# Where a decay scan and a reciprocal stand in the VectorE queue: an RWKV-7 recurrence fused with a feed-forward layer

## The chip, the cores and the metric

The kernel runs on one core of a Trainium2 chip. The metric is the device time of one execution in microseconds (us); smaller is better. A core has five engines that work side by side: PE (TensorE, matrix products, with PEld for the loading of its weights), DVE (VectorE), ACT (ScalarE), POOL (GpSimd) and SP, which here only issues transfers (its queue is written SPq). Each engine works through its own list of instructions, and semaphores tie the lists together. Products land in PSUM, from where DVE or ACT fetch them; everything else lies in SBUF.

## The reference, cut to what matters

The inputs `r, k, v, w, a, b` have the shape (4 batches, 8 heads, 768 steps, 40). For every batch and head a 40 x 40 state is carried over the steps; its outputs, 320 per token for 3072 tokens, then go through a feed-forward layer with a hard-swish.

```python
for t in range(S):
    y[:, :, t] = np.einsum('bhd,bhde->bhe', rt, state)
    Sa = np.einsum('bhde,bhe->bhd', state, at)
    state_decay = state * wt[:, :, None, :] - np.einsum('bhd,bhe->bhde', Sa, bt)
    state = state_decay + np.einsum('bhd,bhe->bhde', vt, kt)
...
h = x @ w_in                        # 3072 x 320 by 320 x 2048
g = h * np.clip(h + 3.0, 0.0, 6.0) / 6.0
return (g @ w_out).astype(np.float32)   # by 2048 x 320
```

## The kernel before, in words

**Units.** The sequence is cut in blocks of 64 steps. A unit is one such block of two batches with all 8 heads; there are 24 (`NK`), worked in groups of four (`NU`). Within a block the recurrence is turned into matrix products. A unit has two parts. The part that needs no state, `prepare` (stages W, gam, A, B, F, factor, K, E, EV), is made well ahead; the part that carries the state, `step` (RT, R, VT, S, U, C, UT, rS, sn, H, y, move, move2), follows in order of the units. Once per group a 64 x 64 triangular system is inverted for all 32 heads of the group: `invert` (L648 to L682) is a chain of some 60 DVE operations named prod (L660) and x (L666), each needing the one before, ending in two transposes tb (L669) and tt (L674).

**W and gam.** Stage W turns a block of decays by PE (L420), ACT copies them into `wm` (L480, L481), and one DVE `tensor_tensor_scan` multiplies them up to running products, `prods` (L484). Stage gam then takes the reciprocal of one half of the products on DVE (L495) into `gam`, and three small POOL copies (L496, L497, L499) bring over the rest. Stage A takes a second reciprocal (L510), later.

**The feed-forward layer.** Each unit gives two jobs, r = 0 and r = 1, one for each half of the 2048 features (the first two units are ordered otherwise). A job has two halves: `expand` multiplies by `w_in` into two PSUM banks named h (L974), and `contract` multiplies the result by `w_out` into a bank named o (L1015). Between them stand ACT (L989) and DVE (L990), which make the tiles gt from h. In expand there are 16 wide products, over 128 rows, and 8 short ones, over 64 rows each, for the last 64 of the 320 inputs. The short ones are held back by `narrow`: where `spread[0]` is set they are issued before a certain recurrence product, or else inside the next contract, before the last of its four pieces (`n == LATEST`, after 6 of its 8 products). Only when the short ones are done are the h banks complete, so only then can L989 and L990 begin; and the next expand needs the same two banks.

**The order.** The order of all instructions is written out by hand; the framework adds only the waits. For units from 8 on (`i >= 2 * NU`) the loop is: `a_block` collects the stages that are due and hands them to `together`, which issues all their PE products first, in the order of `PRODUCTS`, and then, in `finish`, all that follows them on the other engines, in the order of `RESULTS` (W and gam stand third and fourth in it, behind RT and y). Then `feed` issues some pieces of the feed-forward layer by `pieces(1)`, and with each of them some operations of the inversion by `aside`. A stage is a generator: its first `yield` separates its products from the rest.

**The end.** When the recurrence is done, `while jobs or next(stream): next(stream)` runs the jobs that are left. With `spread[0]` still set from the loop, the short products of those jobs are issued inside the contract before. A finished unit leaves as a tile ob (L1033, ACT) in two transfers to HBM (L1038, SPq).

Of the kernel before, what the change touches and what calls it, by code (L numbers as in the profile page):

```python
# [17 lines left out]
BL = 64  # L18
# [11 lines left out]
def kernel(  # L30
# [42 lines left out]
    nc = tc.nc  # L73
# [4 lines left out]
    NU = 2 * NP  # L78
# [16 lines left out]
    def bank(tag, shape, bufs):  # L95
        return ps.tile(shape, F32, name=tag, tag=tag, bufs=bufs)
# [11 lines left out]
    def ps_pair(*dims):  # L108
# [19 lines left out]
        out=ident[:], in_=ones, pattern=[[1, P]],  # L128
# [4 lines left out]
        out=ones[:, 0:BL], in_=ones[:, 0:BL], pattern=[[1, BL]],  # L133
# [3 lines left out]
        out=ones[BL:P, 0:BL], in_=ones[BL:P, BL:P], pattern=[[1, BL]],  # L137
# [240 lines left out]

    PE, DONE = 1, 2
    NK = NG * NU
    names = [(2 * (i // NU) + i % NU // NP, i % NP) for i in range(NK)]
    data = [{} for _ in range(NK)]
# [1 line left out]
    def fetch(name, i, engine=None):  # L386

        if i is None or i >= NK:
            return
        x, crossed = {"W": (w, 0), "A": (a, 0), "B": (b, 0), "K": (k, 0), "R": (r, 1),  # L390
                      "V": (v, 1)}[name]
        if name == "V":
            t = values[i % AHEAD]
        else:
            t = (others if i < 2 * NU and i % 2 and name != "R" else inputs)[name]
        g, p = names[i]
        engine = engine or nc.sync
        for q in range(2):
            y = x[2 * p + q, :, g * BL:(g + 1) * BL, :]
            rows = slice(q * BL, (q + 1) * BL)  # L400
            if crossed:
                for s in range(2):
                    engine.dma_start(out=t[rows, 4 * s:4 * s + 4, 0:D],
                                     in_=y[s::2].rearrange("h t e -> t h e"))
            else:
                engine.dma_start(out=t[rows, :, 0:D], in_=y.rearrange("h t e -> t h e"))
        data[i][name + "N"] = t

    def following(i):

        if i < 2 * NU:

            return i + 2 if i % NU < NU - 2 or i % 2 == 0 else None
        return i + 1

    def turn_pairs(x):

        o = ps_any([P, NPR, P])
        for n in range(NPR):
            nc.tensor.transpose(out=o[:, n, :],  # L420
                                in_=x[:, 2 * n:2 * n + 2, :].rearrange("p s e -> p (s e)"),
                                identity=ident[:])
        return o
# [24 lines left out]
    def half(i, n=SLOT):  # L448
        return slice(SLOT * i, SLOT * i + n)
# [21 lines left out]
    def prepare(i, F):  # L471
        n, o = i % NU, data[i]
        halves = i >= 2 * NU
        def w_stage():
            wt = turn_pairs(o["WN"])
            yield PE

            wv = wm[:].rearrange("p (r m i) -> p r m i", m=2, i=HB + 1)
            x = wt[:].rearrange("p r (q m i) -> p (r q) m i", q=2, m=2)
            nc.scalar.activation(out=wv[:, :, 0, 1:HB + 1], in_=x[:, :, 0, ::-1], func=AF.Copy)  # L480
            nc.scalar.activation(out=wv[:, :, 1, 1:HB + 1], in_=x[:, :, 1, :], func=AF.Copy)  # L481
            fetch("W", following(i))
            prods = o["prods"] = tmp.tile([P, NB, 2, HB + 1], F32, name="prods", bufs=2)
            nc.vector.tensor_tensor_scan(  # L484
                out=prods[:].rearrange("p r m i -> p (r m i)"), data0=wm[:], data1=start[:],
                initial=0.0, op0=ALU.mult, op1=ALU.add,
            )

        def gam_stage():

            gam = o["G"] = grp.tile([P, NPR, P], F32, name="gam", tag="gam", bufs=NU + 2)
            rgam = o["rg"] = tmp.tile([P, NPR, P], F32, name="rgam", bufs=2)
            gv = gam[:].rearrange("p r (q i) -> p (r q) i", q=2)
            rv = rgam[:].rearrange("p r (q i) -> p (r q) i", q=2)
            nc.vector.reciprocal(gv[:, :, 0:HB], o["prods"][:, :, 0, 1:HB + 1][:, :, ::-1])  # L495
            nc.gpsimd.tensor_copy(gv[:, :, HB:BL], o["prods"][:, :, 1, 0:HB])  # L496
            nc.gpsimd.tensor_copy(rv[:, :, 0:HB], o["prods"][:, :, 0, 0:HB][:, :, ::-1])  # L497
            dec = grp.tile([P, 2, 2, NPR], F32, name="dec", tag="dec", bufs=NU + 2)
            nc.gpsimd.tensor_copy(dec[:].rearrange("p m q r -> p r q m"),  # L499
                                  o["prods"][:].rearrange("p (r q) m i -> p r q m i", q=2)[:, :, :, :, HB])  # L500
            o["dec"] = dec
            if i <= 2 * NU:
                fetch("V", i)
            yield from ()
# [434 lines left out]
    narrow, spread, LATEST = [], [False], 2  # L939
# [67 lines left out]
    def contract(i, r, gts):  # L1007
        split = i < SPLIT
        if r == 0 or split:
            op = bank("o", [P, DM], 1)  # L1010
        else:
            op = sums.pop(i)
        for c in range(2):
            for n in range(NQ):
                nc.tensor.matmul(out=op[:], lhsT=gts[c][:, n, :],  # L1015
                                 rhs=wout[:, c * HJ + r * NQ + n, :],
                                 start=((split or r == 0) and c == 0 and n == 0),
                                 stop=((split or r == 1) and c == 1 and n == NQ - 1))
                if n % 2 and (c == 0 or n < NQ - 1):
                    yield True  # L1020
        if r == 0:
            sums[i] = op
            if split:
                part = ffn.tile([P, 3 * P], F32, name="part", tag="xt", bufs=6)[:, 0:DM]
                nc.scalar.activation(out=part, in_=op[:], func=AF.Copy, scale=1.0 / 6.0)
                sums[i] = part
        else:
            ob = ffn.tile([P, DM], F32, name="ob", bufs=OB)
            if split:
                nc.vector.scalar_tensor_tensor(out=ob[:], in0=op[:], scalar=1.0 / 6.0,  # L1030
                                               in1=sums.pop(i), op0=ALU.mult, op1=ALU.add)
            else:
                nc.scalar.activation(out=ob[:], in_=op[:], func=AF.Copy, scale=1.0 / 6.0)  # L1033
            del ready[i]
            g, p = names[i]
            for q in range(2):
                row = (2 * p + q) * T + g * BL
                nc.sync.dma_start(out=out[row:row + BL, :], in_=ob[half(q)])  # L1038
        yield True


# [6 lines left out]
    def pieces(n):  # L1048

        owed[0] += n * (8 / 9 if spread[0] else 1)  # L1050
        while owed[0] >= 1:
            owed[0] -= 1
            if not next(stream):
                owed[0] = 0.0

    def aside(n, weight=0):

        for _ in range(n):
            if side and next(side[0], side) is side:
                side.popleft()  # L1060
            due[0] += weight
            while due[0] >= 1:
                due[0] -= 1
                next(weights, None)
# [116 lines left out]
    for line in PLAN:  # L1181
        plan.append([])
        while line:
            i = line.popleft()
            if i != "T":
                i = int(i)
# [50 lines left out]
    BLOCKS = 4  # L1237
    FIRST_NARROW = PRODUCTS[len(TURNS)]

    def together(stages):  # L1240

        begun, banks = [], 0

        def finish():
            begun.sort(key=lambda x: RESULTS.index(x[0]))
            for _, rest in begun:
                for _ in rest:
                    pass
            begun.clear()
            shared[0] = None  # L1250

        for name in PRODUCTS:
            if name == FIRST_NARROW and narrow and spread[0] and stages:
                narrow[0]()
            for stage in stages.get(name, []):
                if name in TURNS:
                    need = 1
                else:
                    width = WIDTH.get(name, NPR * BL)
                    need = 2 * (shared[0] is None or shared[1] + width > 512)  # L1260
                if banks + need > 5:
                    finish()
                    banks, need = 0, 1 if name in TURNS else 2
                banks += need
                rest = stage()
                next(rest)
                begun.append((name, rest))
        begun.extend((name, stage()) for name in stages if name not in PRODUCTS
                     for stage in stages[name])
        finish()  # L1270
# [26 lines left out]
    def feed(n, inversion):  # L1297

        whole = int(n)
        for k in range(whole):  # L1300
            pieces(1)
            aside(inversion)
        pieces(n - whole)

# [25 lines left out]
    for _ in range(2):  # L1330
        for _ in a_block(m):
            pass
        m += 1
    while jobs or next(stream):
        next(stream)

# [29 lines left out]
```

## Time and profile before

Three runs gave 831.4 us in the median (829.04 to 831.72). The profiled execution took 831.98 us; its span, from the first to the last instruction, is 830.2 us.

| what | value | how to read it |
|---|---|---|
| PE busy | 746.4 us, 90% of the span | matrix products, their ends modelled |
| DVE busy | 547.4 us, 66% | includes the inversion chains |
| ACT, POOL busy | 321.7 us, 156.1 us | 39% and 19% |
| PE busy, 360 to 790 us | 425.44 of 430 us | the steady part |
| DVE busy, 360 to 790 us | 258.71 of 430 us | the steady part |
| scan L484 | 24 times, 1254 ns each | one a unit |
| reciprocal L495 | 24 times, 1741 ns each | one a unit |
| gt on ACT L989, on DVE L990 | 96 times each, 686 and 677 ns | two a job |
| wide h products L974 | 2304 records, mean 284 ns | each fp32 product leaves two records; wide and short mixed; pipelined, so these overlap |

The sixteen units whose preparation the loop issues (8 to 23) have their scans between 264.26 and 633.2 us. Before 240 us the kernel loads and converts weights, and PE is often idle; that stretch is not touched by the change.

### The profile page before, as it was taken

To read this page: it belongs to the slowest core of one execution; us is meant where nothing else is said; L and a number is where in the kernel's file an instruction comes from. 1 tells how busy PE (TensorE), PEld (TensorE's weight loads), DVE (VectorE), ACT (ScalarE), POOL (GpSimd) and SP (SyncE) were. 2 spreads that over 40 slices of the span, in tenths; PEclk is the share of its full clock that TensorE was granted. 3 is DMA by queue.
4 is the path that set the end of the run, shared out by engine and by line. 5 is a ranking of instruction groups with operands and counts; after the bars stand their busy time and mean duration, and the time that the engine had idled before them with its cause. 6 is when DMAs were issued, how large, how long until landed. Compare 5 with 4: busy or idle time off the path is not lost.

```text
span 830.2 us, 35843 instructions
## 1 busy us (share of the span) xinstructions
PE 746.4 (90%) x15832; PEld 632.0 (76%) x15832; DVE 547.4 (66%) x1108; ACT 321.7 (39%) x864; POOL 156.1 (19%) x305
## 2 busy tenths in 40 slices
PE   4732877898999999999999999999999999999997
PEld 3622766686887878788888888878888888888875
DVE  7999697988964769844589654799556685232201
ACT  1323744232344533454433635334553334322211
POOL 3231301122112230321220222112212102000000
PEclk7755587999999999999999999999999999999999
DMA  7573344331133230322331332232232101100000
GB/s 141 85 187 85 91 113 100 70 62 25 21 59 65 52 66 19 59 46 48 56 51 28 60 62 44 42 58 36 45 60 48 22 20 29 29 20 16 15 18 16
DMA packets 174218, 45.05 MB, mean 54 GB/s; under 512 B 157424, under 2 KB 172784, under 8 KB 174064
## 3 DMA queue, kind: packets, MB, share of 16 engines
q1 hardware_dynamic: 171920, 42.44, 26.8%
q8 instruction: 125, 2.05, 1.0%
q10 hardware_dynamic: 2144, 0.33, 0.2%
q14 instruction: 29, 0.24, 0.1%
HBM read 34.08 MB, written 3.93 MB: 46 GB/s over the span
## 4 chain that ended last, share of the span: by engine, by line
PE 70%; DVE 12%; issue 9%; ACT 3%; POOL 2%; DMA 1%; SPq 0%; POOLq 0%; DVEq 0%; ACTq 0%
PE h L974 24%; PE o L1015 22%; PE any L458 4%; PE any L889 3%; PE any L420 2%; PE any L430 2%; PE any L865 2%; DVE prod L660 2%; DVE x L666 2%; PE any L770 1%; PE any L809 1%; DVE parts L320 1%; PE any L830 1%; PE any L846 1%; PE any L696 1%
## 5 line engine op out<-in xcount | busy, mean ns | idle before, releaser
L974 PE MATMUL h<-xt,win 128*128 128x128 f32 (+1 forms) x2304 | 252.8, 284 | 7.0 <-DVE gt L990 7.0
L974 PEld LDWEIGHTS h<-xt,win 128*128 128x128 f32 (+1 forms) x2304 | 232.5, 193 | 25.8 <-issue 8.8
L1015 PE MATMUL o<-wout,gt 128*128 128x320 f32 x768 | 232.8, 445 | 0.2 <-DVE gt L990 0.2
L1015 PEld LDWEIGHTS o<-wout,gt 128*128 128x128 f32 x768 | 139.0, 191 | 51.2 <-issue 1.4
L989 ACT ACTIVATE gt<-h,three 128x512 f32<-128x512 f32 x96 | 62.1, 686 | 104.6 <-PE h L974 104.4
L990 DVE SCALAR_TENSOR_TENSOR gt<-gt,h 128x512 f32<-128x512 f32 x96 | 61.5, 677 | 61.2 <-ACT gt L989 61.2
L660 DVE TENSOR_TENSOR prod<-x 128x30 f32<-128x30 f32 (+9 forms) x180 | 62.8, 349 | 13.5 <-POOL x L651 8.1
L904 POOL TENSOR_TENSOR yg<-ys,gam 128x512 f32<-128x512 f32 x22 | 39.1, 1778 | 167.9 <-DVE ys L902 121.9
L874 DVE TENSOR_TENSOR state<-any,state 40x160 f32<-40x160 f32 (+1 forms) x88 | 27.9, 321 | 62.7 <-PE any L865 36.3
L666 DVE TENSOR_TENSOR x<-x,prod 128x30 f32<-128x30 f32 (+9 forms) x180 | 65.2, 362 | 5.4
L590 POOL TENSOR_TENSOR KBt<-K,rgt 128x320 f32<-128x320 f32 x24 | 21.1, 880 | 248.1 <-ACT rgt L580 217.3
L467 DVE COPY_PREDICATED score<-mask,any 128x256 f32<-128x256 int32 x143 | 53.4, 436 | 4.0 <-PE any L458 3.6
L495 DVE RECIPROCAL gam<-prods 128x256 f32<-128x256 f32 x24 | 41.5, 1741 | 13.5 <-POOL yg L904 13.2
L510 DVE RECIPROCAL rgam<-prods 128x256 f32<-128x256 f32 x24 | 41.8, 1741 | 0.0
L484 DVE TENSOR_TENSOR_SCAN prods<-wm,start 128x528 f32<-128x528 f32 x24 | 30.1, 1254 | 16.6 <-ACT wm L481 14.9
L623 ACT ACTIVATE EV<-any 64x160 f32<-64x160 f32 x92 | 24.8, 295 | 39.8 <-PE any L617 30.3
L902 DVE TENSOR_TENSOR ys<-any,ys 128x256 f32<-128x256 f32 x44 | 16.6, 418 | 34.1 <-PE any L617 18.3
L749 ACT ACTIVATE RT<-any 128x256 f32<-128x256 f32 (+1 forms) x44 | 15.5, 400 | 49.6 <-PE any L430 49.5
L889 PE MATMUL any<-score,KBt 64*64 64x64 f32 x1536 | 31.2, 232 | 2.4 <-DVE score L467 1.6
L889 PEld LDWEIGHTS any<-score,KBt 64*64 64x64 f32 x1536 | 27.5, 144 | 5.3 <-DVE score L467 1.7
L729 ACT ACTIVATE tinv<-any 32x256 f32<-32x256 f32 (+1 forms) x56 | 19.3, 344 | 28.9 <-PE any L719 28.1
L775 DVE TENSOR_TENSOR RR<-any,EV 128x160 f32<-128x160 f32 x44 | 12.2, 318 | 25.6 <-PE any L458 25.4
(193 smaller groups left out, 1077.4 us busy)
## 6 DMA issues: line engine op xcount, KB each, us to landing
B<-in_b_dram SPq DMA_DIRECT2D x48, 80.0 KB
K<-in_k_dram SPq DMA_DIRECT2D x48, 80.0 KB
V<-in_v_dram SPq DMA_DIRECT2D x96, 40.0 KB
out_dram<-ob SPq DMA_DIRECT2D x48, 80.0 KB
R<-in_r_dram SPq DMA_DIRECT2D x92, 40.0 KB
W<-in_w_dram SPq DMA_DIRECT2D x40, 80.0 KB
A<-in_a_dram SPq DMA_DIRECT2D x40, 80.0 KB
xt<-yg SPq DMA_DIRECT2D x72, 40.0 KB
```

The costliest lines, as they stand in the source:

```text
L458: nc.tensor.matmul(out=o[i][half(q), n, :], lhsT=lhs[half(i, D), n ^ (2 * q * swap), half(q)], rhs=rhs[half(i, D), n, half(q)], start=True ...
L467: nc.vector.copy_predicated(out=x[:, 4 * i:4 * i + 4, :], mask=mask4, data=o[i])
L495: nc.vector.reciprocal(gv[:, :, 0:HB], o["prods"][:, :, 0, 1:HB + 1][:, :, ::-1])
L510: nc.vector.reciprocal(rv[:, :, HB:BL], o["prods"][:, :, 1, 1:HB + 1])
L660: nc.vector.tensor_tensor(out=pv, in0=_ap(x[:], (i + 1) * L + i, [[L, n], [0, i]]), in1=_ap(x[:], i * L, [[0, n], [1, i]]), op=ALU.mult,)
L666: nc.vector.tensor_tensor(out=rest, in0=rest, in1=pv, op=ALU.add)
L889: nc.tensor.matmul(out=y[q][half(s), pr, :], lhsT=o[name][half(q), h * D:h * D + SLOT], rhs=m[name][half(q), 4 * rs + 2 * s + j, :], start ...
L904: nc.gpsimd.tensor_tensor(out=yg[:], in0=m["ys"][:].rearrange("p r q t -> p r (q t)"), in1=o["G"][:], op=ALU.mult)
L974: nc.tensor.matmul(out=hp[c][:, i, :], lhsT=lhsT, rhs=rhs, start=(begun[c] == 0), stop=(begun[c] == 3 * NQ - 1))
L989: nc.scalar.activation(out=gt[:], in_=hp[c][:], func=AF.Relu, bias=three[:], scale=1.0)
L990: nc.vector.scalar_tensor_tensor(out=gt[:], in0=gt[:], scalar=6.0, in1=hp[c][:], op0=ALU.min, op1=ALU.mult)
L1015: nc.tensor.matmul(out=op[:], lhsT=gts[c][:, n, :], rhs=wout[:, c * HJ + r * NQ + n, :], start=((split or r == 0) and c == 0 and n == 0), ...
```

## The change

Three edits. First, for units from 8 on, stage W yields a new mark LATER ahead of the scan, and stage gam yields it ahead of its reciprocals and copies. `finish` then lays the rest of the stage aside in `deferred`, and `later()` issues it either after the next `pieces(1)` in `feed` or at the start of the next `together`. Second, `spread[0]` is set to False ahead of the last loop, so that expand issues the 8 short products of a job right behind its 16 wide ones there. Third, the second half of the last unit's output is issued from the ACT queue and no longer from SPq.

```diff
-    PE, DONE = 1, 2
+    PE, DONE, LATER = 1, 2, 3
...
         def w_stage():
...
             fetch("W", following(i))
+            if i >= 2 * NU:
+                yield LATER
             prods = o["prods"] = tmp.tile([P, NB, 2, HB + 1], F32, name="prods", bufs=2)
             nc.vector.tensor_tensor_scan(
...
         def gam_stage():
 
             gam = o["G"] = grp.tile([P, NPR, P], F32, name="gam", tag="gam", bufs=NU + 2)
+            if i >= 2 * NU:
+                yield LATER
             rgam = o["rg"] = tmp.tile([P, NPR, P], F32, name="rgam", bufs=2)
...
             for q in range(2):
                 row = (2 * p + q) * T + g * BL
-                nc.sync.dma_start(out=out[row:row + BL, :], in_=ob[half(q)])
+                queue = nc.scalar if q and i == NK - 1 else nc.sync
+                queue.dma_start(out=out[row:row + BL, :], in_=ob[half(q)])
...
+    deferred = deque()
+
+    def later():
+
+        while deferred:
+            for _ in deferred.popleft():
+                pass
+
     def together(stages):
 
+        later()
         begun, banks = [], 0
 
         def finish():
             begun.sort(key=lambda x: RESULTS.index(x[0]))
             for _, rest in begun:
-                for _ in rest:
-                    pass
+                for at in rest:
+                    if at == LATER:
+                        deferred.append(rest)
+                        break
             begun.clear()
             shared[0] = None
...
         for k in range(whole):
             pieces(1)
+            later()
             aside(inversion)
         pieces(n - whole)
...
+    spread[0] = False
     while jobs or next(stream):
         next(stream)
```

## The prediction, made before the changed kernel was run

> **What bounds the kernel now.** I read the page first: busy shares, then the 40 slices.
>
> ```profile
> PE 746.4 (90%) x15832; PEld 632.0 (76%) x15832; DVE 547.4 (66%) x1108; ACT 321.7 (39%) x864; POOL 156.1 (19%) x305
> PE   4732877898999999999999999999999999999997
> PEclk7755587999999999999999999999999999999999
> ```
>
> PE is full from the tenth slice on, and at full clock. The change touches units 8 to 23 and the end, so only stretches from about 264 us on count. There PE leaves little: 425.44 of 430 us are busy between 360 and 790 us. A gain can only come from PE's idle time, so next I read the waits of PE alone, 240 to 790 us (columns: total us, times, longest).
>
> ```profile
> PE h L974 <- DVE gt L990: 3.6, 3, 1.3
> PE any L458 <- issue: 3.1, 4, 1.0
> PE any L696 <- ACT wm L481: 1.3, 1, 1.3
> PE any L617 <- issue: 1.1, 1, 1.1
> PE any L770 <- DVE score L467: 0.7, 1, 0.7
> PE any L846 <- DVE score L467: 0.2, 1, 0.2
> ```
>
> All of PE's idle time here is 10.6 us. 3.6 + 0.7 + 0.2 = 4.5 us of it waits for DVE; the "issue" rows wait for nothing that the profile shows. The timeline gives the places: L974 idles 1.29, 1.15 and 1.14 us at 308.82, 431.95 and 549.70 us, L770 0.73 us at 312.74, L846 0.20 us at 285.72. The second of them, in the timeline from 426 us:
>
> ```profile
> 426.49 0.75 DVE L902 TENSOR_TENSOR ys<-any,ys 128x256 f32<-128x256 f32 x2
> 427.15 1.25 DVE L484 TENSOR_TENSOR_SCAN prods<-wm,start 128x528 f32<-128x528 f32 x1
> 427.31 2.15 POOL L904 TENSOR_TENSOR yg<-ys,gam 128x512 f32<-128x512 f32 x1 [5.01 <-DVE ys L902]
> 427.95 1.24 ACT L989 ACTIVATE gt<-h,three 128x512 f32<-128x512 f32 x2
> 429.50 1.75 DVE L495 RECIPROCAL gam<-prods 128x256 f32<-128x256 f32 x1 [1.10 <-POOL yg L904]
> 431.17 1.22 DVE L990 SCALAR_TENSOR_TENSOR gt<-gt,h 128x512 f32<-128x512 f32 x2
> ```
>
> The reader is to see that ACT has both gt ready by 429.19, but that DVE reaches them at 431.17: scan, 1.10 us of waiting for POOL's yg, and reciprocal stand ahead. PE waits for the h bank which the first gt frees.
>
> The end is the third view, the timeline from 799 us:
>
> ```profile
> 799.53 1.16 PE L974 MATMUL h<-xt,win 64*128 64x128 f32 x16
> 800.62 1.34 PE L1015 MATMUL o<-wout,gt 128*128 128x320 f32 x4
> 800.73 1.27 ACT L989 ACTIVATE gt<-h,three 128x512 f32<-128x512 f32 x2 [7.40 <-PE h L974]
> 801.44 1.29 DVE L990 SCALAR_TENSOR_TENSOR gt<-gt,h 128x512 f32<-128x512 f32 x2 [11.51 <-ACT gt L989]
> 802.18 3.65 PEld L974 LDWEIGHTS h<-xt,win 128*128 128x128 f32 x32 [0.73 <-DVE gt L990]
> 802.19 3.84 PE L974 MATMUL h<-xt,win 128*128 128x128 f32 x32 [0.22 <-DVE gt L990]
> ```
>
> Behind the short products PE has only 4 records of contract left (about 1.1 us) to cover ACT and DVE, and so waits for the h bank. The same stands at 811.84 us, and at 821.50 us ahead of the last contract.
>
> [...]yg takes 2.15 us beside the scan, but 1.27 us at 787.61 us beside a gt, which has one input in PSUM. [...]the two last transfers start at 826.62 and 827.13 us, and SP's waits for them end at 828.66 and 829.29 us, 2.04 and 2.16 us later.
>
> **The change part by part: the scan.** First what moves. I compared the order of instructions on each engine in both programs. On DVE it differs in five places alone: in two (units 8 and 9) a pair of score copies (L467) comes ahead of scan and reciprocal, in three (units 10, 14 and 18, while an inversion runs) the pair gt L990. For the other eleven units nothing stood between the old place and the new. PE differs in the last three jobs only, POOL nowhere, ACT and SP by the last transfer. POOL's copies L496, L497 and L499 keep their place but wait for the later scan; who needs them (stage A, scale) comes over 8 us later.
>
> - *264 us, unit 8.* DVE would do the scores (0.71 us) when their product ends, about 263.9, in what is now idle time, and the scan 0.3 us later than now. PE has no wait on DVE there (its 0.97 us at 267.14 is "issue"). Gain 0; at most that 0.97.
> - *282 us, unit 9.* The scores come 3 us earlier, and L846's 0.20 us goes. gt starts within 0.1 us of now. PE is the bound until the inversion starts, so I take 0.2, between 0 and 0.2.
> - *304 us, unit 10.* gt's ACT ended at 303.16, so DVE does gt at 304.13, then the scan at 305.35; yg, now beside gt, needs some 1.3 to 1.5 us and is through at about 306, so the reciprocal's wait of 1.09 us shrinks to 0 to 0.25. PE's 1.29 us goes. But what is late next is DVE: from 308 to 343.4 us it runs the inversion without a gap, PE already waits for its score at 312.74, and PE's 1.28 us at 345.27 hangs on the end of the inversion through ACT's L681. So the gain is what DVE gains, 0.85 to 1.09, not 1.29 + 0.73. I take 0.9.
> - *427 us, unit 14.* Here gt's ACT is late: its first half ends at about 428.6. DVE now idles from 427.2 to 428.65 (1.45 us) where it idled 1.10, and then needs gt 1.2, scan 1.25, reciprocal 1.75: the inversion goes on at about 432.8 where it was 432.31, 0.47 us later. PE is released at once and starts 1.15 us earlier, at 430.8. Then it meets the later DVE: L549 at 443.04 needs bt, which ended at 441.58 (margin 1.46; PE 1.15 earlier plus DVE 0.47 later is 1.62, so 0.15 to 0.2 is lost); h at 445.87 needs the gt which ended at 444.65 (margin about 1.1 after 0.1 of signalling, so only 0.6 of PE's lead survives); L696 at 463.61 needs the wm copy which ended at 462.81 and stands on ACT behind the inversion's L681 (margin 0.75: PE's lead can be no more than 0.75 − 0.47 = 0.28). I take 0.3, between 0.25 and 1.15, the upper end if those bounds do not bite.
> - *545 us, unit 18.* The same picture with the same numbers (idle 1.10 and 1.14): 0.3.
>
> Sum: 0 + 0.2 + 0.9 + 0.3 + 0.3 = 1.7 us.
>
> **The short products at the end.** From the chain of waits, a job's PE work there is 3.57 (32 wide records) + 1.14 (16 short) + 16 × 0.269 = 4.31 (contract; 12 take 3.23), together 9.02 us. The period is 811.84 − 802.19 = 9.65 us. With the short ones right behind the wide ones, the whole contract, 4.31 us, lies over ACT and DVE, which need about 2.0 us (800.73 to 802.73). So 0.63 us go at each of two boundaries. At the third, PE's last contract starts 0.22 us after a wait and runs from 821.31 by the chain, 4.85 us with its tail where 4.31 + 0.16 would do, and its predecessor ended at 821.13: 0.6 to 0.7 more. Laid end to end from 792.64: 3 × 9.02 + 4.31 = 31.37, so 824.0 where the last product now ends at 826.07. Gain 2.0 us, between 1.5 and 2.1. The contract adds one wait, for ACT's ob to free the o bank; in the new order wide and short products, 4.7 us, cover it. The short products need the third part of xt. The transfers issued at 792.00 are for unit 23, whose first job is the second of the three; PE comes to its short products at about 805, so nothing is lost.
>
> **The last transfer.** Both halves now start at about the end of ob; the later one started 0.51 us behind. ACT's issue of a transfer was 0.6 to 0.7 us long early in this trace, against 0.47 to 0.60 on SP, so I take 0.5, between 0.3 and 0.6.
>
> Total 1.7 + 2.0 + 0.5 = 4.2 us. Against the profiled execution (831.98, that is a span of 830.2 and 1.8 around it) it gives 827.8. That execution lies 0.58 us above the median of the runs; from 831.4 the forecast is 827.2 us.
>
> **Rivals.** *All waits on DVE go* (4.5 us) with the whole of the end (2.5): 7.0, 824.4 us. For it: the waits are real and are named by the profile. Against it: 0.73 at 312.74 and the margins above; DVE has no gap during inversions. *Only the end gains* and the steady part gives everything back: 2.5, 828.9 us; that would also be the case if the deferral did nothing, which the order of instructions already denies for five of sixteen units. *Slower:* [...]gt now stands with its own wait ahead of scan, reciprocal and inversion. Each us by which ACT's gt comes later than 428.6 delays the inversion by as much, in the three groups of 304, 427 and 545 us. For 0.3% on the slower side the three would have to lose 4.2 + 2.5 = 6.7 us, 2.2 us each beyond the 0.47 counted: about 834.5 us. For it: ACT has four EV copies (1.11 us) ahead of gt. Against it: these start at 426.94, before anything moved, so nothing delays them further.
>
> **How the numbers follow.** About 0.3%, 2.5 us, is what a measurement of this kernel can tell from no change; the three runs spread over 2.7 us. Chances: forecast 0.58, all waits 0.17, only the end 0.18, slower 0.07. The forecast's own bounds are 0 to 0.97 + 0 to 0.2 + 0.85 to 1.09 + twice 0.25 to 1.15, with 1.5 to 2.1 and 0.3 to 0.6, so 3.2 to 7.3 us, or 824.1 to 828.2. Down to 823.5 takes in "all waits" with run-to-run spread, up to 830.0 "only the end" likewise. Faster means below 828.9: nearly all of the first case and the second, under half of the third, some lost to the spread: 0.75. Same: 0.19. Slower: 0.06.
>
> **What would show it.** PE's row "h L974 <- DVE gt L990" gone from the steady part; DVE's first prod or x after the gt at 431.2 coming some 0.5 us later relative to its ys, while PE comes 1.15 earlier; L549, h or L696 then showing new waits on DVE or ACT; yg at 1.3 to 1.5 us in three places; a period of 9.0 us at the end; the two last transfers starting together. Wrong it would be if L696 shows no wait and PE keeps 1.15 us at each place, if DVE waits longer for gt than 1.5 us, or if PE's "issue" waits, 4.8 us here, change their number.

## The result, and the profile after

Fifteen runs of each kernel gave 828.73 us in the median against 832.11 us. The ratio to before, estimated over all these runs and not the quotient of the two medians, is 0.9966 (95% interval 0.9953 to 0.9979), a gain of 2.8 us (1.7 to 3.9). The profiled execution took 827.57 us, its span 825.9 us against 830.2. So the changed kernel is faster, by two thirds of the 4.2 us forecast.

The change moved the code down by a few lines: the scan is L486, the reciprocal L499, h L978, gt L993 and L994, contract L1019, the inversion L664 and L670, tinv's copies L685, the third block's products L700 and L723. Here are the waits of PE in the changed kernel, 240 to 790 us (total, times, longest):

```profile
PE any L458 <- issue: 2.9, 3, 1.3
PE any L774 <- DVE score L467: 1.4, 1, 1.4
PE any L700 <- ACT wm L481: 1.3, 1, 1.3
PE any L621 <- issue: 1.1, 1, 1.1
PE any L850 <- DVE bt L525: 0.9, 2, 0.4
PE any L813 <- issue: 0.5, 1, 0.5
PE any L458 <- ACT UT L841: 0.3, 1, 0.3
```

The row of L974 for gt, 3.6 us before, is gone. What waits for DVE now is L774 at unit 10 (1.4, was 0.7) and, new, L850 for bt, once behind unit 14 and once behind unit 18. DVE's share fell from 4.5 to 2.3 us (1.4 + 0.9). But PE's waits are not all that counts, as the next view shows: four stretches of the changed kernel, cut at the steps of PE's clock (columns: length, PE busy, PEld, DVE, ACT, POOL, granted clock, DMA share, GB/s).

```profile
336.11:339.52 3.41, 3.41 (x127) 3.30 (x122) 3.41 (x2) 1.71 (x2) 1.99 (x3) 1.00 0.32 53
339.52:342.93 3.41, 2.09 (x75) 1.74 (x74) 2.55 (x5) 3.36 (x13) 2.57 (x4) 1.00 0.53 99
342.93:346.35 3.42, 3.42 (x42) 2.97 (x41) 2.48 (x3) 3.20 (x8) 2.05 (x6) 0.50 0.29 48
346.35:349.76 3.41, 3.41 (x88) 2.43 (x88) 2.82 (x6) 0.00 (x0) 0.00 (x0) 1.00 0.52 87
```

PE is fully busy from 342.93 to 346.35, but at half clock (0.50): 42 records, where the two other full stretches shown hold 127 and 88. I call PE's lead the time by which a record of PE starts earlier than the same record does in before. It falls there by 1.17 us, from 3.74 to 2.57. Before had no half clock at all between 200 and 830 us.

A sum over one pair of profiles misleads for another reason. I cut every trace of this study at the same instructions: start-up (to the first product of `any<-at,kt` after 255 us, at 262.89 us in before), steady part (to the first wide product of the last three jobs), end (to the end of the last product), and out (from the end of the last ob to the end of the span). About 0.5 us between end and out is the ob itself.

| profile | start-up | steady | end | out | half clock in the steady part, at |
|---|---|---|---|---|---|
| before | 262.89 | 529.74 | 33.44 | 3.64 | none |
| after | 260.50 | 529.54 | 31.97 | 3.34 | 342.9 |
| after_again | 262.60 | 528.56 | 31.97 | 3.33 | 344.5 |
| tail_only | 263.28 | 531.34 | 31.97 | 3.34 | none |
| tail_again | 263.50 | 531.36 | 31.97 | 3.33 | none |
| defer_only | 261.95 | 528.71 | 33.44 | 3.63 | 344.0 |
| defer_8_to_13 | 263.00 | 528.87 | 31.97 | 3.33 | 311.9 |
| gam_only | 262.74 | 525.32 | 31.97 | 3.33 | 344.7 |
| gam_only_again | 262.77 | 524.99 | 31.97 | 3.33 | 344.9 |
| gam_from_14 | 261.14 | 528.83 | 31.97 | 3.34 | none |
| gam_late_tinv | 264.39 | 525.36 | 31.97 | 3.33 | none |
| late_tinv_again | 262.84 | 524.41 | 31.97 | 3.33 | none |

2.4 of the 4.3 us between the first two spans lie in the start-up, which the change doesn't touch and which varies by 3.9 us over these profiles. The end and the last transfer repeat to 0.01 us: 1.47 and 0.30. The steady part of before happens to be the lowest of three with the same order (530.8 in the mean); four with the deferral, of units 8 to 13 at least, have 528.9. By these the change is worth 1.9 + 1.47 + 0.30 = 3.7 us, within the interval; with 1.6 us between steady parts of the same order, this is rough.

### The profile page after: what moved, and what is told of

Same layout as the page of the kernel before. It is cut to its first block, busy times and chain, and to the rows that moved or that the text cites. A ratio compares the mean times of both kernels' runs of the same rounds, so it can differ in the third digit from the quotient of the medians.

```text
span 825.9 us, 35844 instructions
## 1 busy us (share of the span) xinstructions
PE 744.1 (90%) x15832; PEld 631.8 (77%) x15832; DVE 547.3 (66%) x1108; ACT 320.8 (39%) x864; POOL 153.2 (19%) x305
## 4 chain that ended last, share of the span: by engine, by line
PE 67%; DVE 12%; issue 11%; ACT 4%; POOL 2%; DMA 2%; SPq 1%; POOLq 0%; DVEq 0%; ACTq 0%
PE h L978 22%; PE o L1019 22%; PE any L458 4%; PE any L893 3%; PE any L430 2%; PE any L420 2%; PE any L869 2%; DVE prod L664 2%; DVE x L670 2%; PE any L774 1%; PE any L813 1%; DVE parts L320 1%; PE any L834 1%; PE any L700 1%; PE any L850 1%
## 5 line engine op out<-in xcount | busy, mean ns | idle before, releaser
L978 PE MATMUL h<-xt,win 128*128 128x128 f32 (+1 forms) x2304 | 251.6, 283 | 3.0 <-DVE gt L994 3.0
L978 PEld LDWEIGHTS h<-xt,win 128*128 128x128 f32 (+1 forms) x2304 | 232.4, 192 | 19.0 <-issue 4.2
L1019 PE MATMUL o<-wout,gt 128*128 128x320 f32 x768 | 232.2, 446 | 0.0
L1019 PEld LDWEIGHTS o<-wout,gt 128*128 128x128 f32 x768 | 139.5, 192 | 51.2 <-issue 1.4
L994 DVE SCALAR_TENSOR_TENSOR gt<-gt,h 128x512 f32<-128x512 f32 x96 | 61.6, 677 | 59.4 <-ACT gt L993 59.3
L993 ACT ACTIVATE gt<-h,three 128x512 f32<-128x512 f32 x96 | 62.0, 685 | 96.0 <-PE h L978 95.7
L664 DVE TENSOR_TENSOR prod<-x 128x30 f32<-128x30 f32 (+9 forms) x180 | 62.7, 348 | 13.5 <-POOL x L655 8.1
L670 DVE TENSOR_TENSOR x<-x,prod 128x30 f32<-128x30 f32 (+9 forms) x180 | 65.1, 362 | 5.4
L908 POOL TENSOR_TENSOR yg<-ys,gam 128x512 f32<-128x512 f32 x22 | 36.5, 1658 | 165.7 <-DVE ys L906 99.6
L499 DVE RECIPROCAL gam<-prods 128x256 f32<-128x256 f32 x24 | 41.5, 1741 | 10.5 <-POOL yg L908 9.9
L486 DVE TENSOR_TENSOR_SCAN prods<-wm,start 128x528 f32<-128x528 f32 x24 | 30.2, 1258 | 7.7 <-ACT wm L481 6.0
```

The costliest lines, as they stand in the source:

```text
L664: nc.vector.tensor_tensor(out=pv, in0=_ap(x[:], (i + 1) * L + i, [[L, n], [0, i]]), in1=_ap(x[:], i * L, [[0, n], [1, i]]), op=ALU.mult,)
L670: nc.vector.tensor_tensor(out=rest, in0=rest, in1=pv, op=ALU.add)
L908: nc.gpsimd.tensor_tensor(out=yg[:], in0=m["ys"][:].rearrange("p r q t -> p r (q t)"), in1=o["G"][:], op=ALU.mult)
L978: nc.tensor.matmul(out=hp[c][:, i, :], lhsT=lhsT, rhs=rhs, start=(begun[c] == 0), stop=(begun[c] == 3 * NQ - 1))
L993: nc.scalar.activation(out=gt[:], in_=hp[c][:], func=AF.Relu, bias=three[:], scale=1.0)
L994: nc.vector.scalar_tensor_tensor(out=gt[:], in0=gt[:], scalar=6.0, in1=hp[c][:], op0=ALU.min, op1=ALU.mult)
```

## The experiments

**The two halves.** `tail_only` takes the two `yield LATER` out of the changed kernel, `defer_only` takes the other two edits out.

```diff
--- tail_only against after (the same in gam_stage)
-            if i >= 2 * NU:
-                yield LATER
--- defer_only against after
-    spread[0] = False
...
-                queue = nc.scalar if q and i == NK - 1 else nc.sync
-                queue.dma_start(out=out[row:row + BL, :], in_=ob[half(q)])
+                nc.sync.dma_start(out=out[row:row + BL, :], in_=ob[half(q)])
```

> The end alone: the short products of the last three jobs at once and the second output half from ACT, no deferral. Theory 1 (the deferral is worth about 1.4 us, the end 1.8): 1.8 us below before, ratio 0.9978; in the trace the stretch from the wide products of the first of the three jobs to the last product takes 32.0 us against 33.4, and the steady part shows before's three waits of L974 for gt, about 1.2 us each. Theory 2 (the deferral is worth all of the 4.5 us of waits): also 0.9978, but then the full change must stand at 0.993. Theory 3 (the deferral is worth nothing): the full gain, 2.8 us, ratio 0.9966.

> The deferral alone, with the end as before. Theory 1: 1.4 us below before, ratio 0.9983, with steps of PE's lead of about +0.5 at unit 9, +0.9 at unit 10 and 0 across units 14 and 18. Theory 2: 4.5 us, ratio 0.9946. Theory 3: 1.000. If the 3.4 us at half the PE clock that the changed kernel's trace shows near 342 us belong to the deferral, they are here again and the ratio is about 0.9997.

Measured: tail_only 0.995 (0.9933 to 0.9968, from 6 runs), more than its trace can hold; defer_only 0.9981 (0.9968 to 0.9995, 18 runs). Because of that contradiction tail_only ran again:

> tail_only once more, since its first ratio, 0.995, is below what its trace accounts for (1.8 us, 0.9978). If the trace is right, the two together come nearer to 0.9978; if it is not, they stay at 0.995 and this trace shows a gain elsewhere.

It gave 0.9981 (0.9971 to 0.999, 22 runs): this fits the trace's 1.8 us. The first ratio was then a lucky sample of six; short start-ups are the likely reason, but the runs without a profile don't show theirs. The product of the two halves, 0.9981 × 0.9981 = 0.9962, agrees with the change; with both tail runs weighted by their number it is 0.9955, which still lies in the change's interval. The timeline of tail_only at the end shows how the end's 1.47 us come about:

```profile
794.62 4.83 PE L974 MATMUL h<-xt,win 128*128 128x128 f32 x48
799.37 4.58 PE L1015 MATMUL o<-wout,gt 128*128 128x320 f32 x16
799.48 1.27 ACT L989 ACTIVATE gt<-h,three 128x512 f32<-128x512 f32 x2 [4.17 <-PE h L974]
800.19 1.29 DVE L990 SCALAR_TENSOR_TENSOR gt<-gt,h 128x512 f32<-128x512 f32 x2 [8.28 <-ACT gt L989]
```

ACT and DVE are through at 801.48, and the contract that covers them lasts to 803.9; no idle time stands ahead of any product.

**Units 14 and 18.** `defer_8_to_13` leaves the deferral away from unit 14 on.

```diff
-            if i >= 2 * NU:
+            if 2 * NU <= i < 14:
                 yield LATER
```

> The changed kernel with the deferral only for units 8 to 13. Theory 1 (at units 14 and 18 the deferral is worth nothing): the same time as the changed kernel within 0.3 us, with before's waits of 1.15 us of L974 for gt back at both places and no steps of PE's lead across them, and the half clock near 342 us again. Theory 2 (0.3 us or more at each): 0.6 us or more above the changed kernel.

Measured: 0.9966 (0.9953 to 0.9979), the same as the change. The two waits of L978 for gt are back (2.3 us together) and the time isn't worse, so removing them at units 14 and 18 is worth nothing that these runs can tell; their interval is 1.1 us to either side. The traces say the same more sharply, as the next paragraph shows. Its half clock came at another place, which is taken up below.

**Why they are worth nothing.** The timeline of the changed kernel at unit 14:

```profile
423.90 0.75 DVE L906 TENSOR_TENSOR ys<-any,ys 128x256 f32<-128x256 f32 x2
424.73 1.27 POOL L908 TENSOR_TENSOR yg<-ys,gam 128x512 f32<-128x512 f32 x1 [5.00 <-DMA R<-in_r_dram]
425.36 1.24 ACT L993 ACTIVATE gt<-h,three 128x512 f32<-128x512 f32 x2
426.07 1.28 DVE L994 SCALAR_TENSOR_TENSOR gt<-gt,h 128x512 f32<-128x512 f32 x2 [1.42 <-ACT gt L993]
427.27 1.25 DVE L486 TENSOR_TENSOR_SCAN prods<-wm,start 128x528 f32<-128x528 f32 x1
428.62 1.75 DVE L499 RECIPROCAL gam<-prods 128x256 f32<-128x256 f32 x1
430.29 0.33 DVE L670 TENSOR_TENSOR x<-x,prod 128x220 f32<-128x220 f32 x1
```

DVE stands idle for 1.42 us until ACT's gt is there, and the inversion (L670) goes on 6.39 us after ys began; before it was 432.31 − 426.49 = 5.82. PE's lead rises by 1.39 us at h and is then spent on a DVE that is 0.57 us late. At L850 0.97 us of it go, 0.45 as idle time ahead of the first record and the rest among its records:

```profile
438.76 0.74 DVE L525 TENSOR_TENSOR bt<-any,rgam 128x256 f32<-128x256 f32 x2
439.23 0.96 PE L850 MATMUL any<-RT,S 40*64 40x64 f32 x29 [0.45 <-DVE bt L525]
```

In before the same two stood so:

```profile
440.83 0.74 DVE L521 TENSOR_TENSOR bt<-any,rgam 128x256 f32<-128x256 f32 x2
442.57 0.65 PE L846 MATMUL any<-RT,S 40*64 40x64 f32 x32
```

That is a margin of 0.99 us between the end of bt (441.58) and L846, and 1.39 + 0.57 − 0.99 = 0.97. The rest, 0.44 us, goes at the first of the third block's products (L700), which wait for ACT's wm and the next copy, both standing behind tinv's copies. Behind them the lead over before is 2.53 us; ahead of unit 14 it was 2.57. At unit 18 the steps are 1.37 up, then 0.98 and 0.40 down.

If so, DVE's idle 1.42 us is the place for the scan, which takes 1.25 and needs nothing that is late. `gam_only` leaves the scan where it was and defers only stage gam:

```diff
--- gam_only against after, in w_stage
-            if i >= 2 * NU:
-                yield LATER
             prods = o["prods"] = tmp.tile([P, NB, 2, HB + 1], F32, name="prods", bufs=2)
```

> The changed kernel with the scan left where it was and only gamma's reciprocal and copies deferred. Theory 1 (at units 14 and 18 DVE stands idle 1.4 us for ACT's gt and so resumes the inversion 0.5 us late): the scan, 1.25 us, fills that idle time, the inversion resumes 0.7 to 0.8 us earlier than in before, and PE keeps 0.7 to 1.1 us at each of the two units; together 1.4 to 2.0 us below the changed kernel, about 0.994 of before. Against it: at unit 9 the scores stand behind the scan again, up to 0.3 us back. Theory 2: the same time as the changed kernel within 0.3 us, since gt was not late there. Theory 3: the same as tail_only.

> gam_only once more, beside gam_late_tinv on the same chip, to see which of the two is the faster and whether the half-clock stretch near 342 us comes back. By the traces so far: half clock again behind the wait at the third block, 1.1 us of PE's waits for DVE left, 0.992 to 0.994 of before.

Measured: 0.9923 (0.9904 to 0.9942), and again 0.9934 (0.992 to 0.9948): about 3 us faster than the change, more than the 1.4 to 2.0 expected. The timeline of gam_only at unit 14:

```profile
424.55 0.75 DVE L904 TENSOR_TENSOR ys<-any,ys 128x256 f32<-128x256 f32 x2
425.21 1.25 DVE L484 TENSOR_TENSOR_SCAN prods<-wm,start 128x528 f32<-128x528 f32 x1
426.72 1.29 DVE L992 SCALAR_TENSOR_TENSOR gt<-gt,h 128x512 f32<-128x512 f32 x2 [0.26 <-ACT gt L991]
427.92 1.75 DVE L497 RECIPROCAL gam<-prods 128x256 f32<-128x256 f32 x1
429.58 0.32 DVE L668 TENSOR_TENSOR x<-x,prod 128x220 f32<-128x220 f32 x1
```

Idle 0.26 us and no longer 1.42; the inversion goes on 5.03 us after ys, 0.8 us sooner than before. PE wins 1.39 and 1.38 us at h at the two units and keeps practically all of it, and it waits for DVE 1.1 us in the whole steady part. The expectation took only DVE's 0.8 us for what PE would keep; PE kept more. Of PE's lead at unit 10 gam_only keeps about 0.3 us more than the change, and at unit 9 it loses nothing; why it keeps more at unit 10 stays open.

**The half clock.** The changed kernel once more:

> The changed kernel once more. If the 3.4 us at half the PE clock near 342 us are a matter of the moment, this trace lacks them or has them elsewhere, and PE's lead over before across units 10 to 12 stays at about 0.9; if they belong to the change, they are at the same place and cost 1.2 us again. PE's lead at 262 us, ahead of anything that the change moves, was 2.4 us in the first trace; if it is the state of the start-up alone, it differs here by 1 us or more. Time: 0.9966 of before, give or take 0.0013.

Measured: 0.9959 (0.9944 to 0.9974). The start-up was 2.1 us longer than in the first trace. The half clock was there again behind the same wait of PE for wm at L700, and in defer_only and both gam_only too; in the three traces with the old order it was not.

In the traces of before and after, all 19 changes of the granted clock in each lie whole multiples of 3.413 us apart, to within 0.001 us; in the changed kernel, for one, half clocks begin at 192.74 and at 342.93 us, 44 times 3.413 us apart. Carried on through a trace, these times are a grid; I call its parts of 3.41 us clock stretches and its lines edges. In the clock stretch ahead of the half clock (339.52 to 342.93 above) PE was busy for 2.09 us, 61%.

If the place of the idle time within a clock stretch matters, the lead won at unit 10 has moved the idle 1.3 us to another place. `gam_from_14` is gam_only with `if i >= 14` in gam_stage, so that nothing is shifted there; `gam_late_tinv` is gam_only with the wait itself taken away, by issuing tinv's copies behind the first half of the third block:

```diff
             yield
-            nc.scalar.activation(out=tinv[z:z + L, :, 0:L], in_=tb[z:z + L], func=AF.Copy)
+            copies.append((z, tb))
             nc.gpsimd.tensor_copy(tinv[z + L:z + BL, :, L:BL], tb[z + L:z + BL])
...
         yield DONE
+        for z, x in copies:
+            nc.scalar.activation(out=tinv[z:z + L, :, 0:L], in_=x[z:z + L], func=AF.Copy)
+        copies.clear()
         tp = ps_pair(H, L)
```

> As gam_only, but only for units from 14 on; units 8 to 13 as in before, so that nothing shifts PE against the clock's 3.41 us stretches around 345 us. Clock theory (the half-clock stretch after 342 us comes because the lead won at unit 10 moves PE's idle 1.3 us ahead of L696's third-block products to another place within a stretch): no half clock in the steady part of this trace, no gain at units 9 and 10, 1.3 us kept at each of units 14 and 18, and the end's 1.8: 4.4 us below before, ratio 0.9947. Rival (the half clock belongs to the deferred reciprocal as such, wherever it is): a half-clock stretch at 460 or 580 us, and 1.2 us less.

> gam_only with the two ACT copies tinv<-tb, 2.1 us, issued only ahead of the second half of the third block, so that the wm copies of the next unit no longer stand behind them. Clock theory: PE's wait of 1.29 us at the third block near 345 us goes, and with it the half-clock stretch behind it (1.2 us): 2.4 us below gam_only, about 0.9895 of before. Rival (the half clock has another cause): the wait goes, the half clock stays, 1.2 us below gam_only. If the copies are late for the U products, L809 shows a new wait on ACT and the gain shrinks by it.

> gam_late_tinv once more. Clock theory: no half clock in the steady part again, 1 to 2.4 us below gam_only_again. Rival (its first trace lacked the half clock by chance): half clock in this trace, and no more than 1.2 us below gam_only_again.

Measured: gam_from_14 0.9935 (0.9916 to 0.9954), no half clock, and 1.30 of the 1.39 us of lead won at unit 14 kept. gam_late_tinv 0.9908 (0.9887 to 0.993) and again 0.992 (0.9904 to 0.9935), no half clock in either. From the waits of PE in its second trace:

```profile
PE any L777 <- DVE score L467: 1.1, 1, 1.1
PE any L619 <- issue: 1.1, 1, 1.1
PE any L777 <- ACT zs L708: 0.5, 1, 0.5
PE any L816 <- DVE bt L523: 0.2, 1, 0.2
```

The wait for wm is gone; 0.5 us of it came back as a wait for zs, some more as short waits for bt. On the same chip it stands at 825.0 us against gam_only's 825.88. That is 0.9 us where 2.4 were forecast first and at least 1 the second time, with intervals that overlap, so whether late tinv copies make the kernel faster than gam_only is not settled.

Nor do these two traces show that the wait brings the half clock. PE comes to this place 3.05 and 3.08 us behind an edge there, so that a wait of 1.29 us would have been split by the next edge; in the five traces with the half clock near 343 us the wait began 0.40 to 0.81 us behind an edge. The edges lie differently against the program from one execution to the next, by up to 1.2 us in these traces, as the start-up varies, and that is a rival which no run here excludes.

What sets the half clock off is not settled either. All six cases in the steady parts follow a clock stretch in which PE idled 1.3 us or more and started 9 or fewer feed-forward records. Clock stretches with 1.3 us idle or more and 10 to 12 such records (before, tail_only, tail_again, gam_from_14) had no half clock behind them. That would part the two, if it were not for one of defer_8_to_13 (359.7 us, 1.31 us idle, no such record) without a half clock behind it. Another reading parts all eleven clock stretches: in the six the long wait began 0.4 to 1.2 us behind the edge, in the other five 0.1 or 1.4 to 1.6 us behind it. It was found afterwards, and no run was made to test it. The case of that kernel that did have one:

```profile
308.50:311.91 3.41, 1.98 (x65) 1.72 (x64) 3.17 (x11) 0.22 (x1) 0.00 (x0) 1.00 0.53 104
311.91:315.32 3.41, 3.41 (x53) 3.29 (x46) 3.17 (x11) 0.00 (x0) 0.00 (x0) 0.50 0.24 58
```

It lies behind L774's wait of 1.4 us at unit 10, so the half clock belongs to no one wait. The rival in the expectation of gam_from_14, that a deferred reciprocal brings the half clock wherever it is, fell: there the reciprocals were deferred and none came.

**What the half clock costs.** The same 349 records of PE around unit 10, first in the changed kernel at full clock, then in defer_8_to_13 with the half clock:

```profile
304.23:326.21 21.98, 19.47 (x349) 16.97 (x349) 20.88 (x52) 7.33 (x22) 0.87 (x5) 1.00 0.17 34
306.32:328.49 22.17, 20.74 (x349) 18.27 (x349) 21.07 (x52) 7.35 (x22) 0.87 (x5) 0.92 0.19 37
```

PE is busy for 1.27 us more, but the stretch is only 0.19 us longer. What is gone is the "issue" wait ahead of L621's products (L617 in before), which stands behind this place in all eleven other traces with 1.05 to 1.07 us. Near 343 us it is alike: the "issue" wait of L458 near 363 us, 0.77 to 1.38 us in the seven traces without a half clock near 343, is there in only one of the five with it, the first trace of the changed kernel. The stretch which before runs from 340.05 to 363.79 us takes 24.91 us in that one, 23.90 to 24.04 in the other four, and 23.75 to 24.67 in the seven. So the 1.2 us are lost on balance in the first trace alone. The ratio of defer_only says the same: its expectation had 0.9997 for a half clock that costs 1.2 us; the half clock came, and the ratio was 0.9981. Why the "issue" wait goes is not shown.

## Why the prediction was right, and where not

The direction held, and the time lies in the range, but only because that was widened for the rivals: the forecast's own bounds ended at 828.2 us, and 828.73 was measured. Point by point:

- *What bounds it.* PE, and only its waits can be won: right. The five places were the right ones; the other eleven units show no lasting step above 0.5 us.
- *Unit 8, 0 us:* right. *Unit 9, 0.2 us:* PE's lead rose by 0.52 us in the first trace and as much in the others with the deferral at this unit. The row of waits gave 0.20 for PE's products alone; PEld stood 0.34 us at the same place.
- *Unit 10, 0.9 us:* 1.56 at h, 0.69 given back at L774 for the score. What remains is 0.87, with DVE as the bound and yg through in time, as argued: yg took 1.28 us beside gt where it had taken 2.14 beside the scan.
- *Units 14 and 18, 0.3 us each:* the mechanism was right (idle 1.45 forecast, 1.42 measured; inversion 0.47 us late forecast, 0.57 measured), but the gain was 0. The mis-sized terms are the margins behind the late inversion. At bt 0.15 to 0.2 was forecast and 0.97 lost, because the margin was read at L549 (1.46 us) and not at L846 (0.99), which stands ahead of it; L846 doesn't read bt, yet in the changed kernel its products (L850) wait 0.45 us for it; why is not shown. The other is at L696, where I read a margin of 0.75 us for its first product only. The products fill a pair of PSUM banks, and in the changed kernel there is a second gap among the first of them, 0.2 us, behind the wm wait.
- *The half clock:* in no step of the prediction. It took 1.2 us from PE's lead in the first trace; in the others with it the next "issue" wait fell away and little was lost.
- *The end, 2.0 us:* 1.47. A job took 9.17 us (790.04 to 799.21), not 9.02: the first two records of a contract behind short products lie 0.37 us apart, not 0.27, and the products ahead took 4.75 us rather than 4.71. Three times 0.15 is 0.45 of the missing 0.5; the bounds, 1.5 to 2.1, just missed it.
- *The last transfer, 0.5 us:* 0.30. Both halves start together (822.56), but SP's waits for them end at 824.86 and 824.92, at least 2.3 us later, where starts one behind the other took 2.04 and 2.16. So of the 0.51 us between the two starts some 0.2 were lost to longer transfers; whether because they ran side by side or because of ACT's queue is not shown.
- *Rivals:* "all waits go" (7.0 us) fell, by L774, L850 and defer_8_to_13. "Only the end" (2.5) fell by defer_only. The slower rival rested on ACT's gt coming later than read; it came as read. Its time should be 833.9 us (827.2 + 6.7), not 834.5.
- *Signs and readings:* the "issue" waits do change, from seven to five, which was to be a sign of being wrong; in tail_only, whose steady part is that of before, there are five as well, so it was no sign. PE is full from the eleventh slice on, not the tenth. The yg at 787.61 us, read as standing beside a gt, has it beside it for 0.37 us only; unit 10 of the changed kernel shows the point better.

The total by steps that show: 0.5 + 0.9 − 1.2 + 0 + 1.47 + 0.30 = 2.0 us in the first trace. In the second the steady part gains 1.2 us instead of 0.2, which makes 3.0. The runs have 2.8 (1.7 to 3.9).

## What to carry to other kernels

DVE kept the order of its list here: it stood idle for 1.42 us until ACT's gt was there, with the scan behind it, which in gam_only ran straight behind ys without idle time. So moving work behind an instruction that still has to wait trades its wait for idle time: of the work that stands ahead, leave there what fits into the wait (the scan, 1.25 us into 1.42) and move only the rest. Price a gained wait at the first thing behind it that is late for another engine, and read that margin at every product and for every buffer, not only the first one. And when PE's idle time is moved and not removed, look at its clock afterwards, and then at the whole stretch: what the slower clock takes may come back from a wait that would have stood next (in defer_8_to_13 1.27 us more of busy PE, but 0.19 us more of time).

## What the runs showed of the hardware that was not expected

PE was granted half clock (0.50) for 3.41 us, in six cases, behind a clock stretch with 1.3 us of idle time in it. In defer_8_to_13 it was then busy 1.27 us longer over the same products, but in five of the six cases an "issue" wait of about 1 us that stood next in the other traces was gone, and in these five the half clock cost 0.2 us or nothing that shows. Programs that are idle 1.3 us at the same instruction did or did not meet it; in these traces that went with the place of the wait in the clock stretch, which moved with a gain of 1 us 35 us earlier and with the start-up. The start-up of the same code varied from 260.5 to 264.4 us between executions, which may be why six runs could put a kernel some 2.5 us off (tail_only, 0.995, then 0.9981).
